# Router logits taken off TensorE for seven of nine blocks, and full-height tails in attention

## The chip, the cores and the metric

The kernel is one program on one core of one Trainium2 chip. The metric is the device time of an execution in microseconds (us). Runs of the same kernel agree here within about 1.2 us. The profile is one further execution, recorded by the hardware profiler.

## The reference, cut to what matters

Three stages follow each other, all in float32.

1. Block-causal attention: q, k, v of shape (4 batches, 8 heads, 576 positions, 64). Position block i (64 positions) sees blocks 0 to i; softmax; times v.
2. The result as x (2304 tokens x 512) goes through a squared-ReLU layer: `g = s * relu(x @ w_in)**2 + b`, then `g @ w_out`, with 2048 hidden columns.
3. A top-1 mixture of 8 experts: `logits = x @ w_gate + modality_bias[modality_id]` (w_gate is 512 x 8), the expert is the argmax, its weight the softmax value, and the output is `gate_w * (relu(x @ w1[e]) @ w2[e])`.

## The kernel before

**Attention** goes through 16 units of two heads. For each unit q and k are turned on TensorE (`q_transpose`, `k_transpose`), scores are made block by block, exponentials on ScalarE, the normalising product on GpSimd (line 160), the probabilities turned on TensorE (line 179) and multiplied with v (`pv`, line 202). 576 positions are four chunks of 128 and a tail of 64. The tails of q and k lie in partitions 0 to 63 and are turned by two 64-row transposes (`tails`, line 116). In `pv` the fifth chunk multiplies 64 rows only.

**Squared ReLU** runs in blocks of 256 tokens, nine in all. A *unit of work* is one block with one pair of hidden tiles (256 hidden columns): `hidden` issues 24 matmuls of 256 columns (line 377), then ScalarE takes the ReLU (line 381), VectorE squares (line 382), ScalarE makes the rounded high part `gh` (line 385) and VectorE the low part `gl` (line 386); `project` issues 12 matmuls of 512 columns (line 392). From 150 us on some of this runs beside attention; from about 325 us `after` runs 50 units alone: in iteration n it issues `hidden(n)` and then `project(n - 1)`. The last 36 units are nine blocks with four units each; at the end of a block VectorE collects two rows of 128 tokens x 512 (line 609).

**Router.** When a block is collected, `Router.block` is run as a generator, one step in each of the following four iterations, each step written ahead of that iteration's `project`:

- step 1: eight transposes of the collected rows on TensorE (line 623), two copies out of PSUM
- step 2: four matmuls of the 32-column padded gate against the turned rows (line 631), a copy on ScalarE
- step 3: two transposes back (line 638), then a chain of small VectorE operations to the one-hot of the argmax (lines 641 to 653)
- step 4: two small matmuls that rank the tokens (`pr`, lines 656 and 657), more small VectorE operations, and the rows are written to DRAM

The last block but one runs all its steps at once and is followed by `routed()`: the most frequent expert so far is chosen and its weights and first rows are loaded early (lines 861 and 910). The last block is routed after the loop. Then the experts run.

The build orders each engine's instructions by a planner: of what it holds to be ready it takes what was written first. TensorE, VectorE, ScalarE and GpSimd then execute their lists in order. SyncE's queue carries most transfers.

Of the kernel before, what the change touches and what calls it, by code (L numbers as in the profile page):

```python
# [9 lines left out]
F32 = mybir.dt.float32  # L10
# [3 lines left out]
AF = mybir.ActivationFunctionType  # L14
ALU = mybir.AluOpType
AX = mybir.AxisListType
PSUM = bass.MemoryType.PSUM
P = 128


def attention(nc, tc, ctx, ps, ident, q, k, v, xT_d):
# [7 lines left out]
    B, H, S, D = q.shape  # L29
# [4 lines left out]
    raw = pool("a_raw", 2)  # L34
    vp = pool("a_v", 2)
# [20 lines left out]
    st = {}  # L56
    todo = []

    def load(u, which):
        if u >= NU:  # L60
            return
        b, h0 = u // (H // 2), u % (H // 2) * 2
        ts = st.setdefault(u, dict(raw=[]))["raw"]
        for nm, src in which:
            t = (vp if nm == "v" else raw).tile([P, 5, 2, D], F32, name=f"raw_{nm}", tag=nm)
            for hh in range(2):
                nc.sync.dma_start(t[:, 0:4, hh], src[b, h0 + hh, 0:512].rearrange("(c p) d -> p c d", p=P))
            ps.last["load"] = nc.sync.dma_start(t[0:D, 4], src[b, h0:h0 + 2, 512:].rearrange("h p d -> p h d"))
            ts.append(t)

    def low(scale, out, src, high):
        todo.append((scale, out, src, high))
# [39 lines left out]

    def tails(u):
        t = ps.t.tile([P, 512], F32, name="te", tag="t")
        for n in range(2):
            nc.tensor.transpose(t[:, n * D:n * D + D],
                                st[u]["raw"][n][0:D, 4].rearrange("p h d -> p (h d)"), ident[0:D, 0:D])
        q_high(u, t[:, 0:D], slice(8, 9))
        kh, kl, _ = st[u]["k"]
        nc.scalar.copy(kh[:, 512:], t[:, D:2 * D])  # L120
        low(False, kl[:, 512:], t[:, D:2 * D], kh[:, 512:])
# [67 lines left out]
    def pv(u, grp):  # L189

        s = st[u]
        if grp == 0:
            s["x"] = xo.tile([P, S], F32, name="x", tag="x")
        vt, p = s["raw"][2], s.pop(("pt", grp))
        n = 256 if grp == 0 else 320
        o = ps.o.tile([P, 512], F32, name="o", tag="o")
        cs = range(2) if grp == 0 else range(5)
        for c in cs:
            first, kr = max(0, 2 * c - 4 * grp), P if c < 4 else D
            for hh in range(2):  # L200
                r = slice(hh * D, hh * D + D)
                nc.tensor.matmul(o[r, first * D:n], vt[0:kr, c, hh], p[0:kr, first:, c, r],
                                 start=(c == 0), stop=(c == cs[-1]))
        nc.scalar.copy(s["x"][:, grp * 256:grp * 256 + n], o[:, 0:n])
        if grp == 1:
            b, hp = u // (H // 2), u % (H // 2)
            nc.sync.dma_start(xT_d[hp * P:(hp + 1) * P, b * S:(b + 1) * S], s["x"])
            del st[u]
# [50 lines left out]
class Banks:  # L259
# [3 lines left out]
    def __init__(self):  # L263
        self.last = {}
# [14 lines left out]
class SquaredRelu:  # L279
# [140 lines left out]
    def after(self, ctx, rt, begun, free, routed):  # L420
# [16 lines left out]
        x, rows, px, g = {}, {}, {}, {}  # L437
        x[0] = self.load_x(groups[0][0])
        last, steps = None, iter(())
        for n in range(len(units) + 1):  # L440
            if n < len(units):
                at, p = units[n]
                blk, p0, p1 = groups[at]
                with self.tc.issue_after(self.low_last.ins) if n else nullcontext():
                    next(later, None)
                while p not in self.wo:
                    next(later)
                g[n] = self.hidden(x[at], p)
                if p == p1 - 1:
                    del x[at]  # L450
                if p == max(p1 - 3, p0) and at + 1 < len(groups):
                    x[at + 1] = self.load_x(groups[at + 1][0])
            if last is not None:
                steps = rt.block(*last)
                if last[0] == order[-2]:
                    for _ in steps:
                        pass
                    routed()
                last = None
            next(steps, None)  # L460
            if n == 0:
                continue
            at, p = units[n - 1]
            blk, p0, p1 = groups[at]
            if p == p0:
                rows = rt.rows(blk, self.part_d if p0 else None)
                px = [self.ps_x.tile([P, self.D], F32, name=f"px{t}", tag=f"x{t}") for t in range(2)]
            for t in range(2):
                self.project(px[t], g[n - 1], p, t, p == p0, p == p1 - 1)
            del g[n - 1]  # L470
            if p == p1 - 1:
                rt.collect(px, rows, p0)
                if p1 > half:
                    last = (blk, rows)
                else:
                    for t, r in enumerate(rows):
                        nc.sync.dma_start(self.part_d[blk * TB + t * P:blk * TB + (t + 1) * P], r[:, 0:self.D])
                if at + 1 < len(groups) and groups[at + 1][2] > half >= p1:
                    free()
        return last  # L480


EARLY = 2
PLANNED = 17
TINY = 2
# [15 lines left out]
class Router:  # L501
# [4 lines left out]

    def __init__(self, nc, persist, ident, modality_id, w_gate, modality_bias, x2_d):
        self.nc, self.ident, self.x2_d = nc, ident, x2_d  # L510
# [27 lines left out]
    def setup(self, fix, tmp):  # L538
# [7 lines left out]
        self.wg = t("wgs", [P, 4, 32])  # L546
        nc.gpsimd.memset(self.wg, 0.0)
        nc.scalar.copy(self.wg[:, :, 0:E], wg)
        mb = tt("mb", [P, 2, E])
        nc.sync.dma_start(mb.rearrange("p m e -> p (m e)"),  # L550
                          modality_bias.rearrange("m e -> (m e)").partition_broadcast(P))
# [58 lines left out]
            else:  # L610
                nc.vector.tensor_copy(r[:, 0:D], px[e])

    def block(self, blk, rows):
# [3 lines left out]
        j0 = 2 * blk  # L617
        xf = w("gx", [P, 4, 2, P])
        for e in range(2):
            r = rows[e]  # L620
# [18 lines left out]
        lg, m, m2 = w("lg", [P, 2, E]), w("mx", [P, 2, 1]), w("mx2", [P, 2, 1])  # L639
        bc = lambda a: a.to_broadcast([P, 2, E])  # L640
        nc.vector.tensor_reduce(lg, pl2[:, :, :, 0:E].rearrange("p e c k -> p e k c"), AX.X, ALU.add)
        nc.vector.tensor_add(lg, lg, self.bias[:, j0:j0 + 2])
        nc.vector.tensor_reduce(m, lg, AX.X, ALU.max)
        eq = w("eq", [P, 2, E])
        nc.vector.tensor_tensor(eq, lg, bc(m), ALU.is_equal)
        nc.vector.tensor_mul(eq, eq, bc(self.down))
        nc.vector.tensor_reduce(m2, eq, AX.X, ALU.max)
        n0 = self.seen
        self.seen += 2
        oh = self.oh[:, n0:n0 + 2]  # L650
        nc.vector.tensor_tensor(oh, bc(self.down), bc(m2), ALU.is_equal)
        for n in range(2):
            nc.vector.tensor_add(self.acc[:, n0 + n + 1], self.acc[:, n0 + n], self.oh[:, n0 + n])
        yield
# [167 lines left out]
class Experts:  # L822
# [14 lines left out]

    def open_raw(self, ctx):
        rp = ctx.enter_context(self.tc.tile_pool(name="e_raw", bufs=1, side="right", reuse_waits="tile"))
        self.raw, self.raw_s = ([rp.tile([P, 1024], F32, name=f"raw{a}_{n}") for n in range(8)] for a in range(2))  # L840

    def open(self, ctx):
        def pool(n, b, **kw):
            return ctx.enter_context(self.tc.tile_pool(name=n, bufs=b, reuse_waits="tile", **kw))
        self.sb, self.hp, self.xg, self.ss = pool("e_sb", 2), pool("e_h", 1), pool("e_xg", 4), pool("e_ss", 1)
        wp = pool("e_w", 1)
        self.w1s, self.w2s = ([[wp.tile([P, 1024], F32R, name=f"w{a}{hl}_{n}") for n in range(4)] for hl in "hl"]
# [313 lines left out]
def kernel(  # L1161
# [24 lines left out]
    rt = Router(nc, const, ident, moe2_modality_id, moe2_w_gate, moe2_modality_bias, x2_d)  # L1186
# [32 lines left out]
    def free():  # L1219
        c1.close()  # L1220
        ex.open_raw(c1)

    def routed():
        rt.early()
# [4 lines left out]
    with ExitStack() as c3:  # L1229
# [42 lines left out]
```

## Time and profile before

| what | value |
|---|---|
| median of 3 runs | 922.95 us (922.02 to 923.25) |
| the profiled execution | 923.43 us |
| its span in the profile | 921.7 us |
| TensorE (PE) busy | 894.5 us, 97% of the span |
| VectorE (DVE) busy | 588.6 us, 64% |
| ScalarE (ACT) busy | 520.2 us, 56% |
| GpSimd (POOL) busy | 216.9 us, 24% |
| granted TensorE clock | 0.997 of full speed |

The span begins with the first instruction and ends with the last; 1.7 us of the execution lie outside it. Busy time counts an engine's instructions; PEld is TensorE's weight load, which overlaps its matmuls. [...]

### The profile page before, as it was taken

Reading aid. Unit: us, or ns where it says so; the run is one execution under the profiler, and the core shown is the slowest. Engines: PE = TensorE matmul, PEld = TensorE weight load, DVE = VectorE, ACT = ScalarE, POOL = GpSimd, SP = SyncE. Lnnn points to the kernel's source line nnn. Section 1 sums busy time; section 2 is a strip of 40 time slices with the busy share of each in tenths; the row PEclk is TensorE's granted clock in tenths of the full one; section 3 lists DMA queues with packets and bytes.
Section 4 is the critical chain, followed back from the end, with each engine's and each line's share of the span. In section 5 each row is a group of like instructions: output and inputs, shape, how many; then the busy total and the mean of one; then the engine's idle time right before and its main releaser. Section 6 shows DMA issues by size and latency. Waiting matters only on the chain. (4 is left out here: it accounts for less than half of the span.)

```text
span 921.7 us, 16289 instructions
## 1 busy us (share of the span) xinstructions
PE 894.5 (97%) x5529; PEld 718.4 (78%) x5529; DVE 588.6 (64%) x1368; ACT 520.2 (56%) x1105; POOL 216.9 (24%) x319
## 2 busy tenths in 40 slices
PE   7989999999999999999999999999999999999996
PEld 5666777887878888999988888888467776776775
DVE  5889885464546346777354454446688887676782
ACT  6888795566757543333233223222288786776773
POOL 4676673232333300000000000002024322222111
PEclk9999999999999999999999999999999999999998
DMA  5666543322220233446022211114336696636501
GB/s 142 166 180 171 156 113 85 90 53 75 76 72 27 70 105 103 137 139 205 24 69 69 69 57 59 47 46 161 114 129 243 227 377 236 232 126 246 192 12 38
DMA packets 109477, 113.79 MB, mean 123 GB/s; under 512 B 62679, under 2 KB 80617, under 8 KB 109387
## 3 DMA queue, kind: packets, MB, share of 16 engines
q1 hardware_dynamic: 105579, 100.74, 35.0%
q0 software_dynamic: 3808, 11.94, 3.7%
q8 instruction: 46, 0.75, 0.3%
q14 instruction: 44, 0.36, 0.1%
HBM read 143.58 MB, written 19.80 MB: 177 GB/s over the span
## 5 line engine op out<-in xcount | busy, mean ns | idle before, releaser
L377 PE MATMUL ph<-xh,wih 128*128 128x256 f32 x576 | 163.0, 283 | 0.2 <-ACT r L381 0.2
L377 PE MATMUL ph<-xh,wil 128*128 128x256 f32 x576 | 162.3, 282 | 0.0
L377 PE MATMUL ph<-xl,wih 128*128 128x256 f32 x576 | 162.1, 281 | 0.0
L160 POOL TENSOR_TENSOR p<-p,rc 128x64 f32<-128x64 f32 (+2 forms) x144 | 111.1, 779 | 125.9 <-DVE rc L159 74.5
L381 ACT ACTIVATE r<-ph 128x512 f32<-128x512 f32 x72 | 43.0, 598 | 164.8 <-PE ph L377 139.6
L382 DVE SCALAR_TENSOR_TENSOR r<-r,sc 128x512 f32<-128x512 f32 x72 | 55.8, 775 | 92.9 <-ACT r L381 92.1
L377 PEld LDWEIGHTS ph<-xh,wih 128*128 128x128 f32 x576 | 109.1, 189 | 3.6 <-ACT r L381 0.9
L377 PEld LDWEIGHTS ph<-xl,wih 128*128 128x128 f32 x576 | 109.2, 190 | 2.3
L377 PEld LDWEIGHTS ph<-xh,wil 128*128 128x128 f32 x576 | 109.3, 190 | 0.0
L142 DVE TENSOR_REDUCE nm<-sc 128x1 f32<-128x288 f32 (+8 forms) x160 | 70.6, 451 | 52.3 <-PE sc L140 45.5
L147 ACT ACTIVATE p<-sc,nm 128x288 f32<-128x288 f32 (+8 forms) x160 | 80.7, 508 | 16.9 <-DVE nm L142 5.9
L902 DVE TENSOR_TENSOR w1l<-raw,w1h 128x1024 fp32r<-128x1024 f32 x60 | 71.8, 1224 | 24.7 <-ACT w1h L901 23.0
L392 PE MATMUL px<-woh,gh 128*128 128x512 f32 x200 | 81.6, 408 | 0.0
L392 PE MATMUL px<-woh,gl 128*128 128x512 f32 x200 | 78.6, 394 | 0.0
L902 DVE TENSOR_TENSOR w2l<-raw,w2h 128x1024 fp32r<-128x1024 f32 x64 | 74.7, 1220 | 6.0 <-ACT w2h L901 5.9
L392 PE MATMUL px<-wol,gh 128*128 128x512 f32 x200 | 78.5, 393 | 0.0
L910 POOL DMA_INDIRECT xr<-x_d,gidx_e x2 | 2.3, 1132 | 317.8 <-DMA raw<-in_moe_w_dram 317.5
L901 ACT CAST w2h<-raw 128x1024 fp32r<-128x1024 f32 x64 | 66.5, 1054 | 11.5 <-PE py L999 11.4
L179 PE MATMUL tp<-ident,p 128*128 128x128 f32 x400 | 65.4, 278 | 5.9 <-POOL p L160 4.7
L385 ACT ACTIVATE gh<-r,sc 128x512 fp32r<-128x512 f32 x72 | 52.2, 726 | 32.7 <-DVE r L382 32.6
L901 ACT CAST w1h<-raw 128x1024 fp32r<-128x1024 f32 x60 | 61.7, 1053 | 10.1 <-PE ph L984 8.3
L185 ACT COPY pt<-tp 128x512 f32<-128x512 f32 (+3 forms) x128 | 62.0, 498 | 8.4 <-PE tp L179 7.8
(279 smaller groups left out, 1968.2 us busy)
## 6 DMA issues: line engine op xcount, KB each, us to landing
raw<-in_moe_w_dram SPq DMA_DIRECT2D x172, 512.0 KB
xr<-xT_d SPq DMA_DIRECT2D x19, 512.0 KB
wr<-in_moe_w_in_dram SPq DMA_DIRECT2D x16, 512.0 KB
wr<-in_moe_w_out_dram SPq DMA_DIRECT2D x16, 512.0 KB
row<-part_d SPq DMA_DIRECT2D x20, 256.0 KB
x_d<-row SPq DMA_DIRECT2D x18, 256.5 KB
xT_d<-x SPq DMA_DIRECT2D x16, 288.0 KB
raw_q<-in_q_dram SPq DMA_DIRECT2D x32, 128.0 KB
```

The costliest lines, as they stand in the source:

```text
L142: ps.last["max"] = nc.vector.tensor_reduce(nm[:, e:e + 1], sc[:, 0:w], AX.X, ALU.max, negate=True)
L147: ps.last["exp"] = nc.scalar.activation(pr[:, k0:k0 + w], scs[e][:, 0:w], AF.Exp, bias=nm[:, 0:1], accum_out=sm[:, e:e + 1])
L160: ps.last["scale"] = nc.gpsimd.tensor_mul(pr[:, 0:n], pr[:, 0:n], rc.to_broadcast([P, n]))
L179: nc.tensor.transpose(t[:, e * P:(e + 1) * P], st[u][i][0][:, c * P:(c + 1) * P], ident)
L185: P_COPY(nc, i0)(o, src)
L377: nc.tensor.matmul(ph[:, e], self.wi[p][w][:, c, e * P:(e + 1) * P], x[a][:, c], start=(n == 0), stop=(n == 3 * KC - 1))
L381: nc.scalar.activation(r, ph, AF.Relu)
L382: nc.vector.scalar_tensor_tensor(r, r, self.sc[:, 0:1], r, ALU.mult, ALU.mult)
L385: nc.scalar.activation(gh, r, AF.Identity, bias=self.sc[:, 1:2])
L392: self.nc.tensor.matmul(px, g[a][:, e, t * P:(t + 1) * P], self.wo[p][w][:, e], start=(first and e == 0 and n == 0), stop=(last and e == 1 ...
L901: self.nc.scalar.copy(ws[0][c], r)
L902: self.nc.vector.tensor_sub(ws[1][c], r, ws[0][c].bitcast(F32))
```

## The change

- For seven of the nine blocks (all but the last two in order) the logits are made as dot products without TensorE. The gate is turned once on TensorE at set-up (four transposes), written to DRAM and loaded into all 128 partitions by GpSimd's queue. For each of 2 rows and 8 experts, experts 0 and 4 are one multiply-and-reduce of 128 x 512 on VectorE; the other six are a product of 128 x 512 on GpSimd and a copy with running sum on ScalarE. The 16 dots of a block are issued as 6, 5 and 5 in steps 1 to 3; GpSimd's products have two buffers. Step 4 is as before.
- `project` follows `hidden` at a distance of two units rather than one (`LAG = 2`).
- The tails of q and k share one tile, k's in partitions 64 to 127, and are turned by one 128 x 128 transpose; the lower half of v's fifth chunk is set to zero by GpSimd and `pv` multiplies all 128 rows.
- One of the two sets of raw buffers for expert weights is allocated later.

```diff
         for nm, src in which:
+            if nm == "v":
+                t = vp.tile([P, 5, 2, D], F32, name="raw_v", tag="v")
+                nc.gpsimd.memset(t[D:P, 4], 0.0)
+                tail = t[0:D, 4]
...
     def tails(u):
         t = ps.t.tile([P, 512], F32, name="te", tag="t")
-        for n in range(2):
-            nc.tensor.transpose(t[:, n * D:n * D + D],
-                                st[u]["raw"][n][0:D, 4].rearrange("p h d -> p (h d)"), ident[0:D, 0:D])
+        nc.tensor.transpose(t[:, 0:P], st[u]["tail"].rearrange("p h d -> p (h d)"), ident)
...
-                nc.tensor.matmul(o[r, first * D:n], vt[0:kr, c, hh], p[0:kr, first:, c, r],
+                nc.tensor.matmul(o[r, first * D:n], vt[:, c, hh], p[:, first:, c, r],
...
-        for n in range(len(units) + 1):
+        for n in range(len(units) + LAG):
...
-                steps = rt.block(*last)
+                steps = rt.block(*last, spread=last[0] not in order[-2:])
...
-            at, p = units[n - 1]
+            at, p = units[n - LAG]
...
+LAG = 2
+ON_VECTOR = (0, 4)
...
+    def dots(self, lg, rows, part):
+
+        nc, D, E = self.nc, self.D, self.E
+        for n in part:
+            r, e = rows[n // E], n % E
+            lg_e = lg[:, n // E, e:e + 1]
+            on_vector = e in ON_VECTOR
+            t = self.products.tile([P, D], F32, name="pv" if on_vector else "pg", tag="pv" if on_vector else "pg")
+            if on_vector:
+                nc.vector.tensor_tensor_reduce(t, r[:, 0:D], self.gate[:, e], 1.0, 0.0, ALU.mult, ALU.add, lg_e)
+            else:
+                nc.gpsimd.tensor_mul(t, r[:, 0:D], self.gate[:, e])
+                nc.scalar.activation(t, t, AF.Copy, accum_out=lg_e)
...
+        if spread:
+            for first, last in ((0, 6), (6, 11), (11, 16)):
+                self.dots(lg, rows, range(first, last))
+                if last < 2 * E:
+                    yield
+        else:
+            yield from self.products_of(lg, rows, w)
```

`products_of` holds steps 1 to 3 of before up to the reduction into `lg`; `ranks` holds step 4.

## Rows read from the trace of the kernel before

**Rows 1.** Busy time by stretch: stretch, sum, PE, PEld, DVE, ACT, POOL, clock, DMA.

```profile
0.00:150.00 150.00, 133.49 (x921) 102.83 (x922) 121.78 (x392) 122.33 (x388) 99.71 (x169) 1.00 0.59 154
150.00:325.00 175.00, 174.77 (x1192) 143.99 (x1192) 87.26 (x268) 107.86 (x307) 50.72 (x95) 1.00 0.22 64
450.00:625.00 175.00, 175.00 (x1166) 156.14 (x1165) 82.89 (x246) 49.68 (x85) 0.00 (x0) 1.00 0.19 58
```

**Rows 2.** Timeline of TensorE around one block's router: start, duration, instruction.

```profile
455.42 1.03 PE L623 MATMUL gt<-ident,row 128*128 128x128 f32 x8
456.21 0.48 PE L392 MATMUL px<-woh,gh 128*128 128x512 f32 x1
456.53 0.40 PE L392 MATMUL px<-wol,gh 128*128 128x512 f32 x1
456.76 0.40 PE L392 MATMUL px<-woh,gl 128*128 128x512 f32 x1
...
461.82 0.28 PE L377 MATMUL ph<-xh,wil 128*128 128x256 f32 x1
...
462.60 0.50 PE L392 MATMUL px<-woh,gh 128*128 128x512 f32 x1
...
468.34 0.38 PE L638 MATMUL gl<-ident,lt 128*128 128x128 f32 x2
468.48 0.48 PE L392 MATMUL px<-woh,gh 128*128 128x512 f32 x1
```

**Rows 3.** Timeline of TensorE around one unit's tails.

```profile
174.88 0.39 PE L377 MATMUL ph<-xh,wih 128*128 128x256 f32 x1
175.19 0.27 PE L116 MATMUL te<-ident,raw_q 64*128 64x64 f32 x1
...
175.46 0.38 PE L377 MATMUL ph<-xl,wih 128*128 128x256 f32 x1
175.68 0.28 PE L377 MATMUL ph<-xh,wil 128*128 128x256 f32 x1
175.80 0.28 PE L377 MATMUL ph<-xh,wih 128*128 128x256 f32 x1
```

**Rows 4.** Line 116 from 0 to 150 us: count, duration min/median/max (ns), starts.

```profile
L116 PE MATMUL te<-ident,raw_q x10: 243/271/366, 7.1 to 139.5; 64*128 64x64 f32 x10
```

**Rows 5.** Weight loads of the 64-row form of line 202: busy, mean, idle before.

```profile
L202 PEld LDWEIGHTS o<-pt,raw_v 64*64 64x64 f32 x64 | 3.1, 131 | 4.4 <-issue 4.2 <-DMA raw_q<-in_q_dram 0.3
```

**Rows 6.** What the turn of line 179 waited for, 0 to 150 us.

```profile
  POOL p L160: 13.0, 19
```

**Rows 7.** Durations by line (ns, min/median/max), and one small VectorE group (busy, mean).

```profile
L335 POOL TENSOR_TENSOR wil<-f,wih x8: 1285/1742/1745, 38.7 to 133.0; 128x512 fp32r<-128x512 f32 x8
L335 POOL TENSOR_TENSOR wol<-f,woh x8: 1282/1300/2281, 52.9 to 143.7; 128x512 fp32r<-128x512 f32 x8
...
L147 ACT ACTIVATE p<-sc,nm x160: 310/502/712, 12.1 to 320.1; 128x288 f32<-128x288 f32 x32, 128x64 f32<-128x64 f32 x16, 128x128 f32<-128x128 f32 x16, 128x192 f32<-128x192 f32 x16
L147 ACT ACTIVATION_READ_ACCUMULATOR p<-sc,nm x160: 188/202/272, 12.3 to 320.5; 128x1 f32 x160
...
L382 DVE SCALAR_TENSOR_TENSOR r<-r,sc x72: 729/752/1578, 95.2 to 642.6; 128x512 f32<-128x512 f32 x72
...
L643 DVE TENSOR_REDUCE mx<-lg 128x2 f32<-128x16 f32 x9 | 1.5, 164 | 0.1
```

**Rows 8.** Timeline of GpSimd and of VectorE at 297 us.

```profile
297.63 1.15 POOL L160 TENSOR_TENSOR p<-p,rc 128x576 f32<-128x576 f32 x1 [0.38 <-DVE rc L159]
...
297.75 1.57 DVE L382 SCALAR_TENSOR_TENSOR r<-r,sc 128x512 f32<-128x512 f32 x1
```

**Rows 9.** Weight loads of line 656 in all nine blocks: busy, mean, idle before.

```profile
L656 PEld LDWEIGHTS <-tri 128*128 128x128 bf16 x9 | 0.9, 96 | 1.3 <-DVE oh L651 1.0
```

**Rows 10.** Timeline: GpSimd's first early gather, and TensorE's first use of it.

```profile
640.03 1.26 POOL L910 DMA_INDIRECT xr<-x_d,gidx_e  x1 [317.52 <-DMA raw<-in_moe_w_dram]
...
647.84 0.60 PE L934 MATMUL ptx<-ident,xr 128*128 128x128 f32 x4
```

More of the change, by code (lines that the diff above doesn't have):

```diff
@@ L62, in load @@
         b, h0 = u // (H // 2), u % (H // 2) * 2
-        ts = st.setdefault(u, dict(raw=[]))["raw"]
+        s = st.setdefault(u, dict(raw=[]))
         for nm, src in which:
-            t = (vp if nm == "v" else raw).tile([P, 5, 2, D], F32, name=f"raw_{nm}", tag=nm)
+            if nm == "v":
[3 more added lines that the diff above has]
+            else:
+                t = raw.tile([P, 4, 2, D], F32, name=f"raw_{nm}", tag=nm)
+                if nm == "q":
+                    s["tail"] = raw.tile([P, 2, D], F32, name="raw_t", tag="t")
+                tail = s["tail"][0:D] if nm == "q" else s["tail"][D:P]
             for hh in range(2):
                 nc.sync.dma_start(t[:, 0:4, hh], src[b, h0 + hh, 0:512].rearrange("(c p) d -> p c d", p=P))
-            ps.last["load"] = nc.sync.dma_start(t[0:D, 4], src[b, h0:h0 + 2, 512:].rearrange("h p d -> p h d"))
-            ts.append(t)
+            ps.last["load"] = nc.sync.dma_start(tail, src[b, h0:h0 + 2, 512:].rearrange("h p d -> p h d"))
+            s["raw"].append(t)
     def low(scale, out, src, high):
@@ L198, in pv @@
         for c in cs:
-            first, kr = max(0, 2 * c - 4 * grp), P if c < 4 else D
+            first = max(0, 2 * c - 4 * grp)
             for hh in range(2):
                 r = slice(hh * D, hh * D + D)
-                nc.tensor.matmul(o[r, first * D:n], vt[0:kr, c, hh], p[0:kr, first:, c, r],
+                nc.tensor.matmul(o[r, first * D:n], vt[:, c, hh], p[:, first:, c, r],
                                  start=(c == 0), stop=(c == cs[-1]))
@@ L460, in after @@
             next(steps, None)
-            if n == 0:
+            if n < LAG:
                 continue
-            at, p = units[n - 1]
+            at, p = units[n - LAG]
             blk, p0, p1 = groups[at]
@@ L468, in after @@
             for t in range(2):
-                self.project(px[t], g[n - 1], p, t, p == p0, p == p1 - 1)
-            del g[n - 1]
+                self.project(px[t], g[n - LAG], p, t, p == p0, p == p1 - 1)
+            del g[n - LAG]
             if p == p1 - 1:
@@ L501, with __init__ @@
 class Router:
-    def __init__(self, nc, persist, ident, modality_id, w_gate, modality_bias, x2_d):
-        self.nc, self.ident, self.x2_d = nc, ident, x2_d
+    def __init__(self, nc, persist, ident, modality_id, w_gate, modality_bias, x2_d, gate_d):
+        self.nc, self.ident, self.x2_d, self.gate_d = nc, ident, x2_d, gate_d
         NT = x2_d.shape[0]
@@ L548, in setup @@
         nc.scalar.copy(self.wg[:, :, 0:E], wg)
+        turned = self.ps.tile([P, 4, P], F32, name="gw", tag="g")
+        for c in range(4):
+            nc.tensor.transpose(turned[0:32, c], self.wg[:, c], self.ident)
+        gt = tt("gtmp", [32, 4, P])
+        nc.scalar.copy(gt, turned[0:32])
+        nc.sync.dma_start(self.gate_d, gt[0:E].rearrange("e c p -> e (c p)"))
         mb = tt("mb", [P, 2, E])
@@ L611, in collect, with open_gate, block @@
                 nc.vector.tensor_copy(r[:, 0:D], px[e])
-    def block(self, blk, rows):
+    def open_gate(self, ctx, tc):
+        pool = lambda n, b: ctx.enter_context(tc.tile_pool(name=n, bufs=b, side="right", reuse_waits="tile"))
+        self.gate = pool("r_gate", 1).tile([P, self.E, self.D], F32, name="gate")
+        self.products = pool("r_prod", 2)
+        self.nc.gpsimd.dma_start(self.gate.rearrange("p e d -> p (e d)"),
+                                 self.gate_d.rearrange("e d -> (e d)").partition_broadcast(P))
+    def dots(self, lg, rows, part):
[10 more added lines that the diff above has]
+                nc.scalar.activation(t, t, AF.Copy, accum_out=lg_e)
+    def block(self, blk, rows, spread=False):
         nc, E, D, wk = self.nc, self.E, self.D, self.wk
@@ L617, in block, with products_of @@
         j0 = 2 * blk
+        lg = w("lg", [P, 2, E])
+        if spread:
[3 more added lines that the diff above has]
+                    yield
+        else:
+            yield from self.products_of(lg, rows, w)
+        m, m2 = w("mx", [P, 2, 1]), w("mx2", [P, 2, 1])
+        bc = lambda a: a.to_broadcast([P, 2, E])
+        nc.vector.tensor_add(lg, lg, self.bias[:, j0:j0 + 2])
+        nc.vector.tensor_reduce(m, lg, AX.X, ALU.max)
+        eq = w("eq", [P, 2, E])
+        nc.vector.tensor_tensor(eq, lg, bc(m), ALU.is_equal)
+        nc.vector.tensor_mul(eq, eq, bc(self.down))
+        nc.vector.tensor_reduce(m2, eq, AX.X, ALU.max)
+        n0 = self.seen
+        self.seen += 2
+        oh = self.oh[:, n0:n0 + 2]
+        nc.vector.tensor_tensor(oh, bc(self.down), bc(m2), ALU.is_equal)
+        for n in range(2):
+            nc.vector.tensor_add(self.acc[:, n0 + n + 1], self.acc[:, n0 + n], self.oh[:, n0 + n])
+        yield
+        self.ranks(n0, oh, lg, m, rows, w, bc)
+    def products_of(self, lg, rows, w):
+        nc, E, D = self.nc, self.E, self.D
         xf = w("gx", [P, 4, 2, P])
@@ L638, in block, with ranks @@
             nc.tensor.transpose(pl2[:, e].rearrange("p c k -> p (c k)"), lt[:, e], self.ident)
-        lg, m, m2 = w("lg", [P, 2, E]), w("mx", [P, 2, 1]), w("mx2", [P, 2, 1])
-        bc = lambda a: a.to_broadcast([P, 2, E])
         nc.vector.tensor_reduce(lg, pl2[:, :, :, 0:E].rearrange("p e c k -> p e k c"), AX.X, ALU.add)
[L642 to L654, printed above, removed]
+    def ranks(self, n0, oh, lg, m, rows, w, bc):
+        nc, E, D = self.nc, self.E, self.D
         pr = self.ps.tile([P, 2, E], F32, name="pr", tag="g", padded_shape=[P, 64, E])
@@ L839, in open_raw @@
         rp = ctx.enter_context(self.tc.tile_pool(name="e_raw", bufs=1, side="right", reuse_waits="tile"))
-        self.raw, self.raw_s = ([rp.tile([P, 1024], F32, name=f"raw{a}_{n}") for n in range(8)] for a in range(2))
+        self.raw = [rp.tile([P, 1024], F32, name=f"raw0_{n}") for n in range(8)]
     def open(self, ctx):
@@ L844, in pool @@
             return ctx.enter_context(self.tc.tile_pool(name=n, bufs=b, reuse_waits="tile", **kw))
+        sp = pool("e_raws", 1, side="right")
+        self.raw_s = [sp.tile([P, 1024], F32, name=f"raw1_{n}") for n in range(8)]
         self.sb, self.hp, self.xg, self.ss = pool("e_sb", 2), pool("e_h", 1), pool("e_xg", 4), pool("e_ss", 1)
@@ L1185 @@
     x2_d = dram.tile([NT, D + 1], F32, name="x2_d")
-    rt = Router(nc, const, ident, moe2_modality_id, moe2_w_gate, moe2_modality_bias, x2_d)
+    gate_d = dram.tile([moe2_w_gate.shape[1], D], F32, name="gate_d")
+    rt = Router(nc, const, ident, moe2_modality_id, moe2_w_gate, moe2_modality_bias, x2_d, gate_d)
     part_d = dram.tile([NT, D], F32, name="part_d")
@@ L1221, in free @@
         ex.open_raw(c1)
+        rt.open_gate(cg, tc)
     def routed():
@@ L1228 @@
     rt.open(ctx, tc, ps_g, NT - begun * TB)
-    with ExitStack() as c3:
+    with ExitStack() as c3, ExitStack() as cg:
         last = ffn.after(c3, rt, begun, free, routed)
```

## The prediction

> **What bounds the kernel.** I read the busy shares by stretch first. From 450 to 625 us TensorE is busy for all of 175 us, GpSimd for none and VectorE and ScalarE for less than half; from 150 to 325 us it is 174.8 of 175; only in the first 150 us does it stand idle, for 16.5 us, with the three other engines busy for 100 to 122 us [rows 1]. So wherever router, squared ReLU and late attention run, a microsecond off TensorE is a microsecond of time, as long as nothing that TensorE needs comes later than before. In the first 150 us the pace is shared: 13.0 us of waiting at the turn of the probabilities is put down to GpSimd's normalising product [rows 6]. Then I read TensorE's timeline around the router and the tails for the distance between starts, and durations and waits of the other engines for what takes the work over.
>
> **Router off TensorE.** A hidden matmul normally follows the last after 0.12 us [rows 3], a projection after 0.23 us [rows 2]. Step 1's eight transposes take 455.42 to 456.21, 0.79 us, and the first projection behind them takes 0.32 instead of 0.23 us: 0.88 us. Step 2: from the last hidden matmul at 461.82 to the projection at 462.60 is 0.78 us, less the normal 0.12, plus the same 0.09 behind: 0.75 us. Step 3: 0.14 + 0.09 = 0.23 us [rows 2]. Together 1.86 us a block, seven blocks: **-13.0 us**. Without the 0.09s it would be 1.59 a block, 11.1 us: the lower bound. The gate's four transposes at set-up cost 4 x 0.10 + 0.09: **+0.5 us**, hidden by nothing.
>
> **Tails.** Between the hidden matmul at 174.88 and the next at 175.46 lie 0.58 us instead of 0.12, and that next one takes 0.22 instead of 0.12: 0.56 us for the two 64-row transposes [rows 3]. One full transpose costs 0.10 + 0.09 by the router's: 0.37 us saved a unit. In `pv` the weight loads of the 64-row form stood idle for 4.2 us at issue, 0.26 us for each of 16 units [rows 5]; with 128 rows the form is that of the chunk before. [...] Together 0.63 us a unit. Ten of the 16 tails lie before 150 us [rows 4], six behind. The six count in full, 3.8 us. Of the ten (6.3 us) all may count or nothing; TensorE is busy for 133 of 150 us there but partly waits for GpSimd, which also gets a memset a unit, so I take half: **-6.9 us**, bounds -3.8 and -10.1.
>
> **The longer distance.** A steady TensorE gains nothing from `LAG = 2`, since it waits for nothing now. What it moves is the end: after the last block but one is collected, the early choice of an expert, its weights and its first rows run behind what is left of the squared ReLU, and one `hidden` (24 x 0.12 = 2.9 us) now lies ahead of that collection instead of behind. The first gather is issued at 640.03 and its rows are used on TensorE at 647.84 without a wait [rows 10], so some of these 2.9 us are slack that I can't split. Bounds 0 and +2.9; middle: **+1.5 us**.
>
> **The dots, off TensorE but in front of `pr`.** Each block now has 12 products on GpSimd, 12 copies with sum on ScalarE (0.71 us at most for 512 columns, plus 0.20 for reading the sum [rows 7]: 10.9 us a block) and 4 reductions on VectorE (0.75 each by line 382 [rows 7]: 3 us). A unit is 24 x 0.12 + 12 x 0.23 = 5.7 us, a block 22.7 us, so each engine by itself has room; ScalarE and VectorE were busy 50 and 83 of 175 us [rows 1]. The ReLU may stand behind a copy that waits for GpSimd, but with two units' distance `gl` is needed only two `hidden` and two `project`, 11 us, after its `hidden` ended, and its chain takes about 3 us.
>
> What has no such cover is `pr` in step 4. TensorE executes it in order ahead of a projection, and everything there is queued behind it. It stood close already: in nine blocks its load waited 1.0 us for the one-hot [rows 9]. The first row is collected about 0.5 us before the block's last projection ends (the second row's six matmuls of 0.23 less some 0.9 us of VectorE); `pr` comes three units and one `hidden` later: 3 x 5.7 + 2.9 + 0.5 = 20.5 us. The one-hot is ready after 12 products of p us each, the last copy and hand-over (1.1 us) and nine small VectorE steps (0.16 each [rows 7], 1.5 us): 12p + 2.6. So TensorE stalls for 12p - 17.9 us a block once p is above 1.49, if the planner does not put `pr` later.
>
> GpSimd's product of two 512-column operands took 1.285 us at best; the medians of two groups of eight are 1.742 and 1.300, middle 1.52 [rows 7]. The spread has a visible cause: GpSimd and VectorE exclude each other. At 297.75 line 382 took 1.57 instead of 0.75 us, 0.82 late, while GpSimd's 1.15-us product had started 0.12 us before [rows 8]: VectorE got in 0.21 us before GpSimd's end. So an operation holds the path for its duration less 0.2. With 10 such VectorE operations and one double one in the three units, GpSimd's work takes 12 x 1.08 + 12 x 0.55 = 19.6 us if each meets it: p = 1.64, a stall of 1.7 us. The middle of the measured medians gives 0.3. I take 0.4 a block, **+3 us**; bounds 0 (p = 1.285) and +21 (p = 1.742, 3 us a block).
>
> [...]
>
> **Sum.** 923.43 - 13.0 + 0.5 - 6.9 + 1.5 + 3.0 = 908.5 us for the profiled execution, which lay 0.5 us above the median; I give 908 for the median.
>
> **Rivals.**
> 1. *The products come too late* (the slower side). With p of 1.64 to 1.74 `pr` waits 1.7 to 3.0 us a block, 12 to 21 us: 917 to 926. It decides from the point where the stall eats the 17.9 us that the rest gains: 2.6 us a block, p = 1.70; a VectorE chain of the one-hot stretched by squares and low parts in between would bring this down to 1.6. For it: GpSimd took 1.74 in half of one group, with VectorE at 81%. Against it: VectorE is less than half busy here, and a planner that expects slow products places `pr` later. [...]
> 2. *Everything is covered*: p near 1.3, no stall, all 16 units gain in full, no cost at the end: 923.43 - 13.0 + 0.5 - 10.1 = 901. For it: GpSimd was idle from 450 to 625 us; against: the exclusion of [rows 8].
> 3. *Attention gives nothing early and the end costs fully*: 923.43 - 13.0 + 0.5 - 3.8 + 2.9 + 3.0 = 913. For it: 122 of 150 us on VectorE and ScalarE, 13.0 us of waits for GpSimd, which gets more work.
>
> **Chances.** Forecast (903 to 911): 0.46. Rival 1: 0.30; of these 0.08 still faster, 0.07 within 0.2% (about what a measurement of this kernel can tell, 1.8 us), 0.15 slower. Rival 2: 0.13. Rival 3: 0.11. So faster 0.78, same 0.07, slower 0.15. The range 899 to 925 leaves out most of the slower cases and a little of rival 2; the forecast's own range is 903 to 911.
>
> **What would show it.** TensorE without lines 623, 631 and 638 in seven blocks and a block period of 22.7 to 23.1 us instead of 24.5; its waits at line 656's successor near 3 us in all, put down to the one-hot; GpSimd's products between 1.3 and 1.6 us. Rival 1 shows products of 1.65 and more, and waits at `pr` of over 12 us. The tails show as an attention that ends about 7 us earlier; rival 3 as 4 us, with a gap on TensorE before the early experts. The forecast is wrong above all if GpSimd's product in this stage is not near 1.5 us, or if the planner puts `pr` elsewhere than written.

## The result, and the profile after

The changed kernel takes 936.21 us (median of four runs, 935.51 to 937.09) against 923.10 (922.02 to 923.63) for the kernel before on the same chip: ratio 1.0143, interval 1.0129 to 1.0156. It is 13 us slower, where 908 was forecast; it lies above the whole range. Over all comparisons below the kernel before ran in 922.02 to 925.07 us, a little wider than the 1.2 us given above.

The windows of the changed kernel (stretch, sum, PE, PEld, DVE, ACT, POOL, clock, DMA) answer to [rows 1]; the last line is a short stretch behind one `pr`:

```profile
0.00:150.00 150.00, 132.81 (x916) 104.85 (x917) 122.50 (x384) 122.38 (x388) 98.41 (x172) 1.00 0.59 154
150.00:325.00 175.00, 174.77 (x1204) 146.59 (x1204) 89.66 (x277) 109.15 (x310) 53.33 (x107) 1.00 0.23 64
450.00:625.00 175.00, 159.77 (x950) 141.33 (x949) 134.84 (x255) 91.05 (x218) 117.50 (x79) 0.94 0.16 52
475.60:478.70 3.10, 3.10 (x9) 2.37 (x8) 2.56 (x8) 1.60 (x3) 0.00 (x0) 0.50 0.77 276
```

The first two stretches are as before. The loss is in the third: TensorE, full before, stands idle for 15 us of 175, its granted clock is 0.94 in the mean, and it issues 950 matmuls instead of 1166. Its list of waits in the changed kernel (waiter, releaser, us in total, times, longest) has one line at the router, and it is `pr`:

```profile
PE pr L709 <- DVE oh L673: 15.8, 7, 2.5
```

The block period is the distance between two `pr`. First two lines of TensorE's timeline of the kernel before, then of the changed one with what follows the second `pr` (start, duration, instruction, idle before):

```profile
474.19 0.18 PE L656 MATMUL pr<-oh,tri 128*128 128x16 bf16 x1
498.73 0.18 PE L656 MATMUL pr<-oh,tri 128*128 128x16 bf16 x1
```

```profile
474.10 0.17 PE L709 MATMUL pr<-oh,tri 128*128 128x16 bf16 x1 [2.32 <-DVE oh L673]
...
498.68 0.28 PE L383 MATMUL ph<-xh,wil 128*128 128x256 f32 x1
501.49 0.17 PE L709 MATMUL pr<-oh,tri 128*128 128x16 bf16 x1 [2.53 <-DVE oh L673]
...
502.72 0.57 PE L398 MATMUL px<-wol,gh 128*128 128x512 f32 x1
503.09 0.63 PE L398 MATMUL px<-woh,gl 128*128 128x512 f32 x1
...
505.65 0.63 PE L398 MATMUL px<-woh,gl 128*128 128x512 f32 x1
506.08 0.33 PE L383 MATMUL ph<-xh,wih 128*128 128x256 f32 x1
```

The period went from 24.54 to 27.39 us, where 22.7 to 23.1 was forecast. Two things are to be seen. From the last hidden matmul to `pr` are 2.81 us, of which 0.12 are normal: **2.69 us of standstill**. And behind it projections start 0.43 us apart instead of 0.23; the windows show the granted clock at 0.50 there until some 4.5 us after `pr`. From `pr` to the next hidden matmul are 4.59 us; in a run without standstill, below, 2.90: **1.69 us of low clock and restart**. That run's period is 22.64; the two make 4.38 of the 4.75 us of difference, and 0.37 stays unassigned. The other blocks are much alike but for the seventh: there the standstill is 0.99 us and the granted clock stays at 1.00.

### The profile page after: what moved, and what is told of

Read it like the earlier page. It is cut to its first block, busy times and chain, and to the rows that moved or that the text cites. A ratio compares the mean times of both kernels' runs of the same rounds, so it can differ in the third digit from the quotient of the medians.

```text
span 934.1 us, 16350 instructions
## 1 busy us (share of the span) xinstructions
PE 891.1 (95%) x5391; PEld 718.7 (77%) x5391; DVE 654.1 (70%) x1410; ACT 571.8 (61%) x1260; POOL 345.5 (37%) x420
## 5 line engine op out<-in xcount | busy, mean ns | idle before, releaser
L646 POOL TENSOR_TENSOR pg<-row,gate 128x512 f32<-128x512 f32 x84 | 126.2, 1539 | 99.6 <-ACT gh L391 54.5
L388 DVE SCALAR_TENSOR_TENSOR r<-r,sc 128x512 f32<-128x512 f32 x72 | 62.4, 866 | 44.9 <-ACT r L387 44.6
L647 ACT ACTIVATE pg<-pg 128x512 f32<-128x512 f32 x84 | 52.9, 630 | 57.1 <-POOL pg L646 57.1
L398 PE MATMUL px<-woh,gl 128*128 128x512 f32 x200 | 82.9, 415 | 0.2
L398 PE MATMUL px<-wol,gh 128*128 128x512 f32 x200 | 82.7, 413 | 0.0
L392 DVE SCALAR_TENSOR_TENSOR gl<-r,sc,gh 128x512 fp32r<-128x512 f32 x72 | 56.8, 789 | 24.8 <-ACT gh L391 24.1
```

Source lines behind the costliest of these rows:

```text
L388: nc.vector.scalar_tensor_tensor(r, r, self.sc[:, 0:1], r, ALU.mult, ALU.mult)
L392: self.low_last = nc.vector.scalar_tensor_tensor(gl, r, self.sc[:, 1:2], gh.bitcast(F32), ALU.add, ALU.subtract)
L398: self.nc.tensor.matmul(px, g[a][:, e, t * P:(t + 1) * P], self.wo[p][w][:, e], start=(first and e == 0 and n == 0), stop=(last and e == 1 ...
L646: nc.gpsimd.tensor_mul(t, r[:, 0:D], self.gate[:, e])
L647: nc.scalar.activation(t, t, AF.Copy, accum_out=lg_e)
```

## What stands between the products and `pr`

GpSimd's list, by shape, of the changed kernel (count, minimum/median/maximum ns), and VectorE's reductions:

```profile
L646 POOL TENSOR_TENSOR pg<-row,gate x84: 1279/1736/1818, 451.5 to 632.7; 128x512 f32<-128x512 f32 x84
L644 DVE CUSTOM_DVE_ANT_0 pv<-row,gate x28: 1168/1773/1806, 453.3 to 625.2; 128x512 f32<-128x512 f32 x28
```

The mean product is 1.539 us; the first block's 12 run from 451.52 to 469.72, 1.52 each, the value the prediction took. But the reductions, costed at 0.75 by [rows 7], take 1.77. VectorE's timeline of one block shows more that is late, then the row's collection (line 623), which is not, and then the chain to the one-hot (line 664 to 673):

```profile
479.38 1.25 DVE L719 CAST rlo<-ri 128x2 f32<-128x2 int32 x1
480.55 0.16 DVE L720 CAST rhi<-ri 128x2 f32<-128x2 int32 x1
480.62 0.68 DVE L623 TENSOR_TENSOR row<-px,row 128x512 f32<-128x512 f32 x1
...
488.27 1.77 DVE L644 CUSTOM_DVE_ANT_0 pv<-row,gate 128x512 f32<-128x512 f32 x1
...
489.97 1.77 DVE L388 SCALAR_TENSOR_TENSOR r<-r,sc 128x512 f32<-128x512 f32 x1
...
497.89 0.18 DVE L664 TENSOR_TENSOR lg<-lg,bias 128x16 f32<-128x16 f32 x1 [4.44 <-ACT pg L647]
...
498.49 0.75 DVE L388 SCALAR_TENSOR_TENSOR r<-r,sc 128x512 f32<-128x512 f32 x1
...
499.46 1.22 DVE L321 TENSOR_TENSOR xl<-xr,xh 128x1024 fp32r<-128x1024 f32 x1
500.61 0.74 DVE L392 SCALAR_TENSOR_TENSOR gl<-r,sc,gh 128x512 fp32r<-128x512 f32 x1
501.27 0.17 DVE L673 TENSOR_TENSOR oh<-down,mx 128x16 bf16<-128x16 f32 x1
```

While GpSimd multiplies, reductions and squares that meet it, whose inputs all lie in SBUF (the memory for tiles), end up to 1.1 us late (they take 1.77 instead of 0.68 us in the run without products and 0.75 in [rows 7]), and so does a cast of two columns (1.25 instead of 0.16). The row's collection, one of whose inputs comes from PSUM (the memory for TensorE's results), takes 0.68 us beside products in all seven blocks, as in the run without products. In the chain no operation is late: the last product is over, and VectorE had been idle for 4.44 us. Yet the chain takes 3.5 us instead of 1.5, because a square, an input's low part and a hidden low part (2.5 us) stand within it in VectorE's list. ScalarE's part of these three came late; its timeline:

```profile
497.14 0.63 ACT L647 ACTIVATE pg<-pg 128x512 f32<-128x512 f32 x1 [0.54 <-POOL pg L646]
497.68 0.19 ACT L647 ACTIVATION_READ_ACCUMULATOR pg<-pg 128x1 f32 x1
497.77 0.58 ACT L387 ACTIVATE r<-ph 128x512 f32<-128x512 f32 x1
498.25 1.03 ACT L320 CAST xh<-xr 128x1024 fp32r<-128x1024 f32 x1
```

The ReLU of a hidden pair that ended about 493 stands behind the last summing copy, which waits for the last product. GpSimd's timeline of the same block gives the start and the end of its products (the `gh` named as releaser of the first ends with the row's collection, at 478.7):

```profile
478.81 14.09 POOL L646 TENSOR_TENSOR pg<-row,gate 128x512 f32<-128x512 f32 x9 [9.09 <-ACT gh L391]
493.19 3.91 POOL L646 TENSOR_TENSOR pg<-row,gate 128x512 f32<-128x512 f32 x3 [0.29 <-ACT pg L647]
```

So the standstill adds up: products 18.29 us (478.81 to 497.10), the last copy and hand-over 0.79 (to 497.89), the chain 3.60 (to `pr` at 501.49), less the 19.99 us after which the last hidden matmul (498.68 and 0.12) leaves TensorE free. That is 2.69 us.

## Experiments: the parts

**Tails, transposes alone.** Before, with the shared tile, one transpose and the zeroing, but `pv` still with 64 rows:

```diff
-        for n in range(2):
-            nc.tensor.transpose(t[:, n * D:n * D + D],
-                                st[u]["raw"][n][0:D, 4].rearrange("p h d -> p (h d)"), ident[0:D, 0:D])
+        nc.tensor.transpose(t[:, 0:P], st[u]["tail"].rearrange("p h d -> p (h d)"), ident)
```

> The kernel before with the tails' part of the change alone. Theory A (the tails save TensorE time, and outside the first 150 us all of it counts): 3.8 to 6.9 us faster than before, 916 to 919. Rival B (attention's early part is paced by the other engines, and the saving there is nothing; the order of the rest shifts a little): 2 to 4 us faster, 919 to 921. Rival C (the tails cost, by the extra memset in front of GpSimd's product): 923 or more, and the loss of the whole change would lie here.

922.71 us against 923.27, ratio 0.999 (0.9981 to 0.9999). By 139 us the units' transposes start 1.7 us later than before (141.13 instead of 139.47), and by 271 us 0.9 us of that is won back. This run holds half of the tails' change; the whole follows below.

**Distance of two alone** (before with `LAG = 2`):

> The kernel before with project two units behind hidden, and nothing else. Theory A (the distance is neutral: TensorE waits for nothing in the middle, and the early choice of an expert still has cover at the end): within 1 us of before, 922 to 924. Rival B (the cover at the end is gone): 1.5 to 2.9 us slower, 925 to 926, with TensorE waiting ahead of the early experts.

924.08 against 923.27, ratio 1.001 (1.0001 to 1.0019): it costs 0.8 us.

**Tails, whole**, with `vt[:, c, hh], p[:, first:, c, r]` in `pv`:

> The kernel before with all of the tails' change: shared tile and one transpose for q and k, zeroed lower half of v's chunk, and 128 rows in pv (the first run on the tails held the 64-row form in pv still: its weight loads show 64*64, and the idle before them is 10.2 us as before). Theory A (only the units behind 150 us gain, 0.63 us each, and the memset in GpSimd's queue costs up to 1 us early): 919.5 to 921, last pv near 327 us instead of 329.8, weight-load idle at issue down by 4 us. Theory B (the forecast, half of the early units gain too): 916 to 917. Theory C (the 64-row form costs nothing that counts): 922 to 923.

920.13 against 922.87, ratio 0.9971 (0.9961 to 0.9981): -2.7 us. Weight loads of `pv` in this run, which answer to [rows 5], and GpSimd's wait ahead of the zeroing:

```profile
L208 PEld LDWEIGHTS o<-pt,raw_v x448: 132/137/137, 17.7 to 327.1; 128*64 128x64 f32 x150
  issue: 6.0, 27
```

```profile
POOL raw_v L67 <- PE o L208: 7.5, 7, 3.8
```

The 64-row form is gone and 4.3 us of weight-load idle with it (10.3 before in all of `pv`), as forecast. But the ten early units bring nothing: the transposes of the unit near 139.4 us start at 139.34 instead of 139.47. What sets the pace there is not shown; the zeroing does wait in GpSimd's list for `pv` to free v's buffer, ahead of normalising products. Six late units at the 0.60 us that this trace gives would make 3.6 us, the upper end of the interval (1.8 to 3.6).

## Experiments: the wait at `pr`

**Step 4 behind the projections** of its iteration:

```diff
-            next(steps, None)
+            if not behind:
+                next(steps, None)
...
+            if behind:
+                next(steps, None)
             if p == p1 - 1:
```

> The changed kernel with step 4 (the ranks) of the seven blocks written behind that iteration's project rather than ahead of it, so that TensorE's list has pr 2.8 us later. Theory A (all of the loss is TensorE standing at pr for 2.7 us a block, and the lower clock that follows costs 1.6 us a block): both go, 7 x 4.3 = 30 us less, 906 to 912; waits at pr below 2 us in all, clock 1.00 throughout. Rival B (GpSimd, VectorE and ScalarE are behind by themselves, and pr only shows it): the wait moves to another place, the time stays above 925.

940.43 against 923.27, ratio 1.0197 (1.018 to 1.0215): no gain over the changed kernel. The wait at `pr` is gone, and others stand in its place (TensorE's waits of this run, 440 to 640 us):

```profile
PE px L398 <- ACT gh L391: 11.0, 12, 1.1
PE px L398 <- DVE row L629: 5.9, 4, 1.5
PE px L398 <- DVE gl L392: 3.8, 6, 0.6
```

So `pr` is not the only one that meets the lateness: `gh`, the row and `gl` come late as well, although VectorE is busy for 134 and ScalarE for 89 of the 175 us from 450 on.

**24 transposes ahead of `pr`**, to keep the clock up:

> The changed kernel with 24 transposes of the identity (2.4 us, result unused) on TensorE ahead of pr in the seven blocks: they fill the standstill and take no work away. Theory A (the clock falls because TensorE stood still): clock 1.00 throughout and 7 x 1.6 = 11 us less, 923 to 927. Rival B (the fall has another cause, or is only a consequence of slower issue after pr): the clock still falls, 934 to 938.

948.56 against 923.27, ratio 1.0275 (1.0259 to 1.0291). The granted clock is 1.00 in the whole stage, and waits at `pr` of up to 1.2 us are left, so the low clock does go with the standstill; but the fill costs more than it saves and moves other instructions (the period is 29.2), so the clock's price is not measured by it.

**Copies behind the high part.** ScalarE's summing copies are kept behind `gh` of their iteration's unit, so that no copy stands ahead of a ReLU; with two, then with four product buffers, then with step 4 behind the projections as well:

```diff
-                nc.scalar.activation(t, t, AF.Copy, accum_out=lg_e)
+                with self.tc.issue_after(self.high_last.ins):
+                    nc.scalar.activation(t, t, AF.Copy, accum_out=lg_e)
```

> The changed kernel with each part's copies on ScalarE kept behind gh of the unit of its step (four copies after each ReLU and gh, rather than five, two and five around one ReLU), GpSimd's products still in two buffers. Theory A (ScalarE's list is the cause: the planner places 12 copies where GpSimd needs 18 us, and two ReLUs stand behind copies that wait for GpSimd): the ReLUs come in time, but two buffers make GpSimd wait for the copies; 920 to 930. Rival B (GpSimd and VectorE, which exclude each other, are the pace themselves, whatever ScalarE's list): 934 to 942.

> The same with four buffers for the products. Theory A: GpSimd runs through; what is left is pr ahead of project, which still waits 2 to 3 us a block for the one-hot: 915 to 930. Rival B: no better than the changed kernel, 934 to 942.

> The same with four buffers, and step 4 written behind that iteration's project. Theory A: no engine in front of TensorE is late any more; a block takes 22.7 to 23.5 us, 906 to 916. Rival B: the wait only moves again, as it did when step 4 alone was moved (940); 930 to 942.

Against 923.89: 963.2 (ratio 1.0423, 1.0404 to 1.0441), 944.3 (1.0222, 1.0186 to 1.0258) and 931.96 (1.0091, 1.0073 to 1.0109). With two buffers `pr` waits up to 6.4 us, with four up to 4.0, with the later step 4 still up to 2.1. But GpSimd stops for the copies in all three (63.3, 28.6 and 25.1 us in all), which the second expectation had ruled out. So the three runs don't test the ReLUs' place in ScalarE's list by itself: kept behind `gh`, the copies hold up the products. Without moving step 4 this makes the kernel slower still, and with it 4 us are won of some 30.

## Experiments: how many products, and what of them does the harm

**Four, six and eight experts on VectorE**, one line each (`ON_VECTOR = (0, 2, 4, 6)`, `(0, 1, 2, 4, 5, 6)`, `tuple(range(8))`), so 8, 4 and no products a block instead of 12:

> The changed kernel with experts 0, 2, 4 and 6 on VectorE and the other four on GpSimd with ScalarE: 8 products and 8 copies a block, 8 reductions on VectorE. Theory A (the copies that wait for GpSimd are the cause): four products of 1.52 us less in front of the ReLUs and of the one-hot, 6 us a block, so the standstill goes: 906 to 916. Rival B (the path that GpSimd and VectorE share is full): a product off GpSimd is a reduction more on VectorE, 1.75 us when it meets a product; VectorE is late instead, 925 or more.

> The changed kernel with 6 of 8 experts on VectorE, so 4 products a block on GpSimd. Theory A (what is left of the loss with 8 products is the exclusion, and it goes down with the products): between the run with four experts and that with eight, 912 to 918. Theory B (VectorE is now the pace: 11.6 + 12 x 0.68 + some 5 operations late by 1 us = 24.8 us a block): period 24 to 25, total 919 to 925.

> The changed kernel with all 16 dots as multiply-and-reduce on VectorE; GpSimd and ScalarE get none. Theory A (the mutual exclusion of GpSimd and VectorE and the copies behind it are the price): reductions near 0.7 us, 16 x 0.7 = 11.2 us a block beside some 11.6 us of VectorE's other work, 22.8 us against TensorE's 22.7: no wait at pr, period 22.8 to 23.3, total 909 to 914. Theory B (the reductions are slow by themselves when VectorE is full): 1.4 us and more each, VectorE needs 34 us a block, total over 960.

| products a block | us | against | ratio (interval) |
|---|---|---|---|
| 12 (the change) | 936.21 | 923.10 | 1.0143 (1.0129 to 1.0156) |
| 8 | 918.99 | 923.89 | 0.9946 (0.9928 to 0.9964) |
| 4 | 905.86 | 922.87 | 0.9822 (0.9808 to 0.9835) |
| 0 | 906.34 | 922.87 | 0.9823 (0.9810 to 0.9837) |

The window from 450 to 625 us of the run without products, its reductions, and two of its `pr`, the first with the hidden matmul that follows:

```profile
450.00:625.00 175.00, 174.96 (x1143) 158.14 (x1142) 153.21 (x506) 48.19 (x78) 0.00 (x0) 1.00 0.20 62
```

```profile
L644 DVE CUSTOM_DVE_ANT_0 pv<-row,gate x112: 680/684/690, 452.5 to 601.1; 128x512 f32<-128x512 f32 x112
```

```profile
494.49 0.18 PE L709 MATMUL pr<-oh,tri 128*128 128x16 bf16 x1
...
497.39 0.28 PE L383 MATMUL ph<-xh,wih 128*128 128x256 f32 x1
...
517.13 0.18 PE L709 MATMUL pr<-oh,tri 128*128 128x16 bf16 x1
```

With four or none the kernel is 17 us faster than before; these are the fastest of all runs, and faster than either theory of theirs had it. With 8 the time lies between the two theories. All 112 reductions of the run without products take 0.68 us. VectorE does 16 of them a block, four times those of the change, is busy for 153 of 175 us, and still TensorE waits for nothing (0.2 us in all): the period is 22.64, and the same with four products. With 8 products the period is 24.5 and TensorE waits for `gl` (6.1 us in six waits) and `gh` (2.7): VectorE is busy for 165.5 of 175 us there, since of 8 reductions a block five take about 1.77.

**No products removed, only the copies.** First two of 12 summing copies are kept (the last of each row), then none; the logits left out are columns of the row (the diff is that of the second run):

```diff
+            if e == 0:
+                nc.vector.tensor_copy(lg[:, n // E], r[:, 0:E])
...
-                nc.scalar.activation(t, t, AF.Copy, accum_out=lg_e)
```

> The changed kernel with all 12 products on GpSimd but only two of the 12 summing copies on ScalarE (the last expert of each row); the logits of the experts left out are taken from the first columns of the row by one small VectorE copy, so that the choice of expert is another one. Theory A (copies that wait for GpSimd stand in front of the ReLUs in ScalarE's list; late ReLU chains stretch the chain to the one-hot): ReLUs on time, chain to the one-hot 2 us or less, wait at pr under 1 us a block, period 22.8 to 23.6, total 908 to 916. Theory B (12 products and VectorE's operations beside them are too long whatever ScalarE does): pr or a projection still waits 2 us a block or more, period over 25, total over 922.

> The changed kernel with all 12 products on GpSimd and none of the 12 summing copies on ScalarE; the logits of those six experts are the first columns of the row, so the choice of expert is another one, and times are read from the stage of the blocks alone (starts of pr). Nothing waits for GpSimd any more, and only the mutual exclusion with VectorE is left of the products. Theory A (the exclusion alone, through VectorE's list in order, makes the block long): period still over 24 us, with waits of projections for gh and gl. Theory B (ScalarE's list, where a copy that waits for a product stands ahead of a ReLU, and the lateness of the last product make it long): period 22.6 to 23.2, no wait of TensorE over 0.3 us a block, although VectorE's reductions take 1.7 us.

The times, 963.22 against 922.87 (ratio 1.0436, 1.0420 to 1.0452) and 971.62 against 923.29 (1.0532, 1.0516 to 1.0548), hold a longer end from another choice of experts, so the blocks alone are read: periods 27.5 to 29.0 us with two copies, 28.0 to 29.2 with none. With two, a copy still stood ahead of a ReLU and waited 8.66 us for its product, so that run decides nothing. With none, nothing waits for GpSimd at all, and yet TensorE waits up to 3.0 us a block for `gl`. Its longest line of waits, and VectorE's and ScalarE's timelines of this run:

```profile
PE px L398 <- DVE gl L392: 20.9, 7, 3.0
```

```profile
517.51 1.77 DVE L646 CUSTOM_DVE_ANT_0 pv<-row,gate 128x512 f32<-128x512 f32 x1
...
519.21 1.77 DVE L388 SCALAR_TENSOR_TENSOR r<-r,sc 128x512 f32<-128x512 f32 x1
520.90 1.25 DVE L665 TENSOR_TENSOR lg<-lg,bias 128x16 f32<-128x16 f32 x1
522.18 0.17 DVE L666 TENSOR_REDUCE mx<-lg 128x2 f32<-128x16 f32 x1
522.39 0.99 DVE L668 TENSOR_TENSOR eq<-lg,mx 128x16 f32<-128x16 f32 x1
523.30 0.16 DVE L725 TENSOR_TENSOR ex<-lg,mx 128x16 f32<-128x16 f32 x1
523.41 1.21 DVE L669 TENSOR_TENSOR eq<-eq,down 128x16 f32<-128x16 f32 x1
524.66 0.17 DVE L670 TENSOR_REDUCE mx<-eq 128x2 f32<-128x16 f32 x1
524.74 0.74 DVE L392 SCALAR_TENSOR_TENSOR gl<-r,sc,gh 128x512 fp32r<-128x512 f32 x1
```

```profile
510.32 0.60 ACT L387 ACTIVATE r<-ph 128x512 f32<-128x512 f32 x1 [3.64 <-PE ph L383]
521.02 0.72 ACT L391 ACTIVATE gh<-r,sc 128x512 fp32r<-128x512 f32 x1 [10.10 <-DVE r L388]
```

The ReLU is early; ScalarE then waits 10.1 us for a square that stands in VectorE's list behind four reductions of 1.77 us. Of these 10.1 us, 5.4 are the lateness of the four reductions and the square itself (4 x 1.09 and 1.02). So the lateness beside products is enough to make the block long in the list that the planner made for this run. No run has the changed kernel's own list without the lateness, so its share there stays open.

**Writes in place of products**: for 11 of the 12 products of a block GpSimd writes 1664 zeros per partition, 1.49 us, and reads nothing:

```diff
-                nc.gpsimd.tensor_mul(t, r[:, 0:D], self.gate[:, e])
+                if n == 1:
+                    nc.gpsimd.tensor_mul(t, r[:, 0:D], self.gate[:, e])
+                else:
+                    nc.gpsimd.memset(wide, 0.0)
```

> The changed kernel with 11 of the 12 products of a block replaced by a write of 1664 zeros per partition on GpSimd, some 1.5 us each by the 0.92 ns a column of the set-up's writes, so GpSimd's time and ScalarE's 12 copies stay, but GpSimd reads nothing; the logits of those experts are zero plus bias, so the choice of expert is another one, and times are read from the blocks' stage alone. The planner orders ScalarE's copies later here (groups of three between ReLUs). If such writes don't exclude VectorE, the reductions take 0.7 us. Theory A (the exclusion is the harm): then the period is 22.6 to 23.5 with a wait at pr under 1 us a block. Theory B (the last product's lateness and the copies on ScalarE are the harm whatever VectorE does): period 25 or more, with pr waiting over 2 us a block.

999.79 us against 923.29 with the longer end (ratio 1.0846, 1.0821 to 1.0870); the blocks alone have periods of 23.1 to 29.6 us, three of six near 24.7, and `pr` waits 6.3 us in four waits. VectorE's timeline and list of reductions:

```profile
503.78 4.12 DVE L724 CAST rlo<-ri 128x2 f32<-128x2 int32 x1
```

```profile
L646 DVE CUSTOM_DVE_ANT_0 pv<-row,gate x28: 672/680/686, 452.8 to 611.4; 128x512 f32<-128x512 f32 x28
```

Beside writes the reductions take 0.68 us, but a cast is held for 4.1 us (5.5 in the next block), and the row's sum behind it with it. So this run takes the exclusion away from some operations and sharpens it for others, and it settles neither theory: how much the copies and the late last product would cost without any exclusion stays open.

**Six experts on VectorE, distance one** (`LAG = 1`):

> The run with six experts on VectorE (4 products a block), but project again one unit behind hidden instead of two. Theory A (the longer distance costs 0.8 us as it did alone, and nothing waits at a projection): 904.5 to 906. Theory B (the distance covers VectorE's late squares and low parts, which the exclusion still makes late): projections wait 0.5 us a block and more, 908 to 915.

920.02 against 923.29, ratio 0.9964 (0.9951 to 0.9978), where the distance of two gave 0.9822; period 24.3 instead of 22.6; it is slower than both theories had it. TensorE's waits from 440 to 640 us:

```profile
PE px L398 <- ACT gh L391: 4.2, 7, 1.8
PE px L398 <- DVE gl L392: 2.8, 7, 0.4
```

So the distance, neutral alone, is worth some 13 us as soon as VectorE is loaded with dots.

## Why the prediction was wrong

- **Router off TensorE, right.** 1.86 us a block was forecast; without products the period falls from 24.54 to 22.64, 1.90.
- **The dots in front of `pr`: the step that failed.** The stall was sized at 0.4 us a block, +3.0 in all; it measures 2.69 in a full block and 16.9 over the seven. The product was right at 1.52 us, in part by luck: the value was the middle of two set-up groups, while here six or seven of 12 products take 1.74 or more and most of the others 1.3. Wrong was the chain behind the products, nine small VectorE steps at 1.5 us: it takes 3.6 to `pr`, with a square and two low parts in between, which rival 1 had named. The last hidden matmul also left TensorE free 20.0 us after the first product began, not 20.5, and the last copy and hand-over take 0.8 instead of 1.1. So of the 2.69 us, 0.4 are the products as forecast, 2.1 the chain, and 0.5 less 0.3 the rest. No run keeps the chain together in VectorE's list, so what that alone would give is not measured. The prediction used the exclusion of [rows 8] only to lengthen GpSimd's products; it did not charge the same lateness to VectorE, where the four reductions alone take 4 x 1.77 = 7.1 us instead of 3, and casts and squares wait too. In the changed kernel VectorE's idle time ahead of the chain takes this up; with 8 products, and in the run without copies, it reaches TensorE. "VectorE is less than half busy here" is an answer to a load, not to a list in order with late operations in it.
- **What a standstill costs, missing.** No term stood for the clock: 1.6 to 1.7 us a block in six of the seven blocks, some 10 us. Without it the time would have been some 926, by this estimate, just above the range.
- **ReLU behind a copy: half right.** With two units' distance TensorE's list of waits in the changed kernel has no projection, as argued. What was late came between the products and the one-hot instead. And in the run without copies it is VectorE's list that does the harm.
- **Rival 1** named the place and, in a half sentence, the stretched chain. Its price was 917 to 926, since it had no term for the clock either and took p for the cause; p stayed at 1.52. A reduction is 1.77 - 0.68 = 1.09 us late beside products of 1.28 at best, some 0.2 less than their length, as beside the product of [rows 8]. In the table of products 12 of them cost 30 us against none, 936 against 906, while four cost nothing.
- **Tails.** Forecast -6.9, bounds -3.8 and -10.1; measured -2.7, outside these bounds. The prices were about right (0.34 and 0.26 us a unit in the trace, 0.37 and 0.26 forecast); half of the early units was too much, it is none.
- **The longer distance**: +1.5 forecast, +0.8 measured alone; that it also covers late VectorE work was not seen.

With the measured terms (the gate's 0.5 stays as forecast; no run has it alone) and no stall the sum is 923.4 - 13.3 + 0.5 - 2.7 + 0.8 = 908.7; the runs with four products and none lie 2 to 3 us below it, and where these come from stays open. With the stall of 16.9 and some 10 for the clock it is some 936, against 936.22 for the profiled execution. That these meet so closely is luck in part, since the open 2 to 3 us and the unassigned 0.37 a block nearly cancel in it.

## What to carry to other kernels

Before work is moved to an idle GpSimd, charge its operations to VectorE too: here a reduction with both inputs in SBUF ended 1.09 us late beside two-input products of 1.28 at best, and what stood behind it in the list with it. Before work is put in front of a step that TensorE executes in order, look at what else the lists of the other engines hold between the two: here 2.5 us of other VectorE work stood in a chain priced at 1.5. Here 16 reductions on a VectorE that ends 88% busy cost nothing, and 4 of them beside 12 products cost 30 us (936 against 906). And a stall on TensorE cost more than its length: here 2.7 us of standstill were followed by 1.7 us of low clock.

## What the runs showed of the hardware

- In the changed kernel TensorE stood still for 2.5 us up to `pr` at 474.10; from 475.60 to 478.70 its granted clock was 0.50, and projections started 0.43 us apart instead of 0.23.
- Beside two-input products VectorE's reduction of two operands (0.68 us alone) takes 1.77, its two-input operations of 16 columns up to 1.25 instead of 0.17, and a cast of two columns 1.25 instead of 0.16. The row's collection, with one of its two inputs in PSUM, is not late (0.68), and the one-input TENSOR_REDUCE took 0.17 both times (as did one of the two-input operations, so this is no proof). Beside writes the two-operand reduction is not late (0.68) and the cast is, by 4 us: it took 4.12 us and ended with the second of two writes (1.49 each) that followed a product. Why the cast is late there and the reduction not, no run shows.
